# The a*b product of batch 1 rewritten as Strassen's seven block products

## Chip, cores and metric

One core of one Trainium2 chip runs the whole program. The metric is device time in microseconds (us), the median of several runs. TensorE (PE in the rows; its weight loads are PEld), VectorE (DVE), ScalarE (ACT) and GpSimd (POOL) each work through their own queue in order; SyncE (SP) issues the transfers.

## What is computed

An attention layer over 2 batches of 576 tokens, 8 heads of 64, gives x (1152 x 512). Then follow a bilinear layer and a mixture of four experts:

```python
a = x @ w1            # 512 -> 1024
b = x @ w2
h = a * b @ w3        # 1024 -> 1024
x = h @ w_out         # 1024 -> 512
for e in range(4):
    out += p[:, e:e+1] * (np.maximum(x @ e_w1[e], 0) @ e_w2[e])
```

Everything is float32. The kernel reaches that with products of float32r halves: a value is split into a high part (a copy to float32r) and a low part (the value less its high part), and each product is made of three passes, low by high, high by low and high by high (`PASSES`, line 54). The high part is a copy on ScalarE or GpSimd, the low part a subtraction by `lo_dve` (line 107, VectorE) or `lo_pool` (line 104, GpSimd).

## The kernel before

The work comes in four stretches. **Stretch 1** holds the attention of both batches (eight pairs of heads, p = 0 to 3 for batch 0, 4 to 7 for batch 1), the product of w3 and w_out (`wacc`, line 471) and a*b of batch 0 (`b0`, line 596). Its order is written out by hand in the list `FIRST` (lines 19 to 48), where each word is a part: `s`, `t`, `v`, `n`, `z` are TensorE's work for attention, `w` and `b` that for the weights' product and for a*b, the others are the conversions between on the other engines, `@` a load. `manual_schedule` (line 660) keeps every engine's queue in that order. The parts `z4` to `z7` transpose batch 1's attention output into PSUM; `zh4` to `zh7` copy it as the high part (line 398, ScalarE), `zl4` to `zl7` subtract for the low part (line 401, VectorE).

**Stretch 2**, the last words of `FIRST` (`k00_0` to `kc31`), is c of batch 0: hT (a*b split in two) times the product of w3 and w_out, 192 matmuls of line 615, with copies to `x2` (line 624).

**Stretch 3** is a*b of batch 1 (`b1`, lines 664 and 814 to 828): 16 units u, unit 2m for the m-th block of 128 columns of w1 and 2m+1 for that of w2, each times the two halves of 288 tokens over four blocks of 128 of the depth (line 541; 12 matmuls for a unit and half, 384 in all). The weights come back from DRAM, where batch 0 stored them as float32 (`wf`, lines 512 and 527), and are split by ScalarE and VectorE (line 532). An even unit's result is copied by ScalarE (`keep`, line 551); for an odd one VectorE multiplies (`times`, line 555), ScalarE copies the high part of hT (line 560), VectorE subtracts for the low part. The two banks are M0 and M1. c of batch 1 for the first 320 tokens (`c1`, lines 830 to 836) comes behind in the program, in banks o0 to o3, and was put by the scheduler between the units, 12 matmuls at a time.

**Stretch 4** is the four experts, whose first layer is already done by Strassen's seven products (`step`, lines 910 to 954, products of line 923). Its weights are prepared by `prep_1` (line 735): the high parts by ScalarE (line 751), the low parts and the four sums by GpSimd (lines 754 to 764).

The on-chip memory of attention (pools A1 and A2) is given up at line 666, and the pool `px` of stretch 4 takes its place.

## Time and profile before

| | |
|---|---|
| median of 3 runs | 694.44 us (694.14 to 694.61) |
| profiled execution, its own time | 694.88 us |
| its span, first to last instruction | 693.0 us |
| instructions | 12797 |
| busy in the span: PE, PEld | 98%, 88% |
| busy in the span: DVE, ACT, POOL | 60%, 54%, 51% |
| TensorE's granted clock | 1.000 of full speed throughout |

The profile is of one execution. Busy time is the time in which an engine had an instruction running; matmuls overlap, so a busy PE is not yet a PE at its full rate. In the rows further down, a line number is that of the code above, `x24` is a count of instructions, and the text in brackets behind an instruction is the idle time of its engine ahead of it and who ended it.

### The profile page before, as it was taken

The page shows a single profiled execution, that of the slowest core. Times are in us where ns is not written, and L with a number is a line of the kernel's source. Part 1 is how long each engine was busy: PE and PEld are TensorE (multiplying, and loading weights), DVE is VectorE, ACT ScalarE, POOL GpSimd, SP SyncE. Part 2 cuts the span into 40 slices and gives each one's busy share as a digit, 9 for nine tenths or more (in the row PEclk, how much of TensorE's full clock was granted, in tenths as well). Part 3 has the DMA queues.
Part 4 walks back from the last instruction along what each step waited for, and adds up shares of the span by engine and source line. Part 5 has one row for each costly group of instructions (what it writes and reads, how often), then busy time and mean ns, then how long its engine had stood idle before and what let it go on. Part 6 is the DMA issues. An engine that isn't in the chain of part 4 may idle for free.

```text
span 693.0 us, 12797 instructions
## 1 busy us (share of the span) xinstructions
PE 682.0 (98%) x4925; PEld 611.7 (88%) x4925; DVE 416.7 (60%) x784; ACT 370.8 (54%) x785; POOL 354.4 (51%) x350
## 2 busy tenths in 40 slices
PE   8999999999999999999999999999999999999997
PEld 5777798888999999999899998889999898999896
DVE  6788788998851144457766563456563465544563
ACT  6896787576741234355454544445544545544551
POOL 2034645565530001416777766668765668666660
PEclk9999999999999999999999999999999999999999
DMA  9556265534540014112222331231323132313401
GB/s 283 180 160 217 72 197 183 175 108 125 180 138 31 1 61 130 54 61 93 69 85 78 105 122 62 68 116 63 121 83 100 61 111 72 123 61 94 164 31 61
DMA packets 43404, 74.53 MB, mean 108 GB/s; under 512 B 14416, under 2 KB 14416, under 8 KB 43344
## 3 DMA queue, kind: packets, MB, share of 16 engines
q1 hardware_dynamic: 43344, 73.72, 32.9%
q8 instruction: 39, 0.64, 0.4%
q14 instruction: 21, 0.17, 0.1%
HBM read 67.15 MB, written 6.55 MB: 106 GB/s over the span
## 4 chain that ended last, share of the span: by engine, by line
PE 87%; DVE 6%; ACT 3%; DMA 2%; issue 1%; POOL 0%; SPq 0%; ACTq 0%; DVEq 0%; POOLq 0%
PE o L876 28%; PE Z L923 14%; PE ab L541 13%; PE c L615 7%; PE Q L923 7%; PE wacc L471 6%; PE R L923 3%; PE a L329 2%; PE pt L306 2%; PE sc L252 2%; ACT P L273 1%; DVE P L268 1%; DMA wr<-in_moe_w_tiles_dram 1%; DMA qd<-in_q_cols_dram 1%; PE b L363 1%
## 5 line engine op out<-in xcount | busy, mean ns | idle before, releaser
L104 POOL TENSOR_TENSOR w<-r,w 128x512 fp32r<-128x512 f32 x96 | 130.5, 1360 | 188.4 <-ACT w L751 183.2
L876 PE MATMUL o<-w,he 128*128 128x512 f32 x864 | 224.0, 392 | 0.0
L876 PEld LDWEIGHTS o<-w,he 128*128 128x128 f32 x864 | 153.6, 188 | 23.8
L541 PE MATMUL ab<-xT,ws 128*128 128x288 f32 x768 | 108.0, 297 | 2.1 <-POOL ws L104 1.7
L861 ACT ACTIVATE he<-t 128x320 fp32r<-128x320 f32 (+1 forms) x96 | 42.7, 445 | 121.0 <-DVE t L952 73.5
L541 PEld LDWEIGHTS ab<-xT,ws 128*128 128x128 f32 x768 | 103.1, 188 | 4.2 <-POOL ws L104 2.6
L862 DVE SCALAR_TENSOR_TENSOR he<-t,he 128x320 fp32r<-128x320 f32 (+1 forms) x96 | 57.2, 595 | 49.1 <-ACT he L861 49.1
L107 DVE TENSOR_TENSOR w<-r,w 128x512 fp32r<-128x512 f32 x64 | 66.5, 1040 | 0.0
L945 DVE TENSOR_TENSOR t<-u,Q 128x320 f32<-128x320 f32 (+1 forms) x32 | 14.6, 455 | 82.8 <-ACT u L943 82.7
L751 ACT CAST w<-r 128x512 fp32r<-128x512 f32 x96 | 58.9, 614 | 0.0
L615 PE MATMUL c<-hT,W 128*128 128x288 f32 (+2 forms) x384 | 52.9, 295 | 0.0
L615 PEld LDWEIGHTS c<-hT,W 128*128 128x128 f32 x384 | 51.6, 188 | 0.0
L923 PE MATMUL Z<-X0T,w 128*128 128x320 f32 x288 | 50.3, 310 | 0.3 <-ACT s L933 0.3
L923 PEld LDWEIGHTS Z<-X0T,w 128*128 128x128 f32 x288 | 46.2, 188 | 4.2 <-ACT s L933 0.7
L471 PE MATMUL wacc<-wo,w3s 128*128 128x512 f32 x192 | 48.2, 400 | 0.0
L923 PEld LDWEIGHTS Z<-X1T,w 128*128 128x128 f32 x288 | 41.0, 189 | 4.0
L471 PEld LDWEIGHTS wacc<-wo,w3s 128*128 128x128 f32 x192 | 35.0, 188 | 8.8 <-issue 1.0
L923 PE MATMUL Z<-X1T,w 128*128 128x256 f32 x288 | 42.1, 282 | 0.0
L268 DVE CUSTOM_DVE_ANT_0 P<-sc,mask 128x128 f32<-128x128 f32 (+4 forms) x72 | 33.7, 515 | 10.9 <-PE sc L252 6.4
L781 ACT CAST w<-r 128x512 fp32r<-128x512 f32 x64 | 39.5, 618 | 0.0
L273 ACT ACTIVATE P<-P,mn 128x128 f32<-128x128 f32 (+4 forms) x72 | 37.5, 579 | 1.2 <-DVE mn L268 1.1
L101 POOL TENSOR_SCALAR w3s<-tf_l 128x512 fp32r<-128x512 f32 x16 | 12.5, 780 | 45.3 <-DVE tf_l L137 34.3
(136 smaller groups left out, 1157.0 us busy)
## 6 DMA issues: line engine op xcount, KB each, us to landing
r<-in_moe_w_tiles_dram SPq DMA_DIRECT2D x64, 256.0 KB, 3.6
r<-in_moe_w_dram SPq DMA_DIRECT2D x64, 256.0 KB, 3.1
w3r<-in_moe_w_tiles_dram SPq DMA_DIRECT2D x16, 512.0 KB, 3.6
wr<-in_moe_w_tiles_dram SPq DMA_DIRECT2D x16, 512.0 KB, 4.0
wor<-in_moe_w_out_dram SPq DMA_DIRECT2D x8, 512.0 KB, 4.3
wf<-tf SPq DMA_DIRECT2D x16, 256.0 KB, 4.2
wr<-wf SPq DMA_DIRECT2D x16, 256.0 KB, 2.9
qd<-in_q_cols_dram SPq DMA_DIRECT2D x8, 352.0 KB, 4.1
```

Of the source, the lines that this page charges most:

```text
L104: nc.gpsimd.tensor_sub(dst, src, r32(hi))
L107: nc.vector.tensor_sub(dst, src, r32(hi))
L268: nc.vector.tensor_tensor_reduce(out=Pt[i, x], in0=src, in1=mask[:, 0:S] if i == NB else mask[:, S + P - w : S + P], scale=ISCALE, scalar= ...
L273: nc.scalar.activation(Pt[i, x], Pt[i, x], AF.Exp, bias=one, scale=-1.0)
L471: nc.tensor.matmul(wacc[u], lhsT=w3s[u][:, a, c, :], rhs=wo[4 * g + c][:, bb, :], start=(c == 0 and x == 0), stop=(c == 3 and x == 2),)
L541: nc.tensor.matmul(ps[:, 0:HS], lhsT=self.ws[u][:, wi, kk, :], rhs=xT[b, kk][:, xi, a * HS : (a + 1) * HS], start=(n == 0), stop=(n == 3 * ...
L615: nc.tensor.matmul(st["ps"], lhsT=Wt[kk][:, wi, d * P : (d + 1) * P], rhs=hT[kk][:, xi, t0 : t0 + tw], start=(kk == 0 and x == 0), stop=(k ...
L751: return lambda: nc.scalar.copy(st["w"][i][:, 0], src(i))
L861: nc.scalar.activation(h[:, 0], src, AF.Relu)
L862: nc.vector.scalar_tensor_tensor(out=h[:, 1], in0=src, scalar=0.0, in1=r32(h[:, 0]), op0=ALU.max, op1=ALU.subtract)
L876: nc.tensor.matmul(o_ps[i], lhsT=h_of[s][x][:, a, i * P : (i + 1) * P], rhs=w2s[s][x][:, b, :], start=first, stop=last,)
L923: nc.tensor.matmul(ps, lhsT=w1s[s][a][:, wi, kk, :], rhs=X[c, b][:, xi, kk, :], start=first and kk == 0 and x == 0, stop=(kk == 1 and x == ...
```

## The change

a*b of batch 1 is computed as Strassen's seven products of 2 x 2 blocks. For each m the left block matrix is made of the m-th columns of w1 and w2, each cut in two along the depth (A11, A12 from w1, A21, A22 from w2); the right one of x, cut in two along the depth and in two along the tokens. Each product is two blocks deep, three passes each, on 288 tokens: 6 matmuls; seven products make 42 for each m, 336 in all. Results are gathered in Z, Q and R (`b1_prods`): three copies by ScalarE (`keep`), three sums by VectorE (`add`), then two multiplications, one copy of the high part (576 wide) and one subtraction for the low part (`fin_h`). Even m use banks M0, M1 and o0, odd m o1, o2 and o3.

The weights are prepared by the `prep_1` of stretch 4 with other arguments: four high parts on ScalarE, four low parts and the two sums of `s24` on VectorE, the two sums of `s31` still on GpSimd. Three sets of tiles are used in turn; the sets for m = 0 to 2 and all of x's blocks (`x_b1`) are made beside c of batch 0 (stretch 2 behind the word `rl71`), two pieces of work behind each word of c; the sets for m = 3 to 7 within the loop, set m+2 beside the products of m from m = 1 on. Batch 1's attention output is now kept as float32 (`xf`), so `zl4` to `zl7` go.

`FIRST` is written anew: the same parts but for those four, in another order. In stretch 1 the loads of weights keep their order but for a few places, `w8` to `w10` come ahead of `s61`, and `z7` comes between `b15_0` and `b15_1`. Only the expert blocks X1B11 and X1B21 (256 tokens) are still split early; X0B11, X0B21 and the first expert's weights follow behind the last products, since their memory is lent to the products.

```diff
 
 
     raw_t, qk_t, phi_t, prob_t = {}, {}, {}, {}
+    xf = []
     halves = (slice(0, SB), slice(SB, P))
 
     mz = A1.tile([P, G, 2, D + 1], F32, name="mz")
@@ -380,8 +381,8 @@
             nc.gpsimd.tensor_add(st["q"], st["q"], st["m"])
 
         def fin():
-            if b:
-                xT[b, h // 2] = main.tile([P, 2, S], F32R, tag=f"g{p}", name=f"xT{b}_{h // 2}")
+            if b and h % 4 == 0:
+                xf.append(main.tile([P, 2, S], F32, tag=f"g{H // 2 + len(xf)}", name=f"xf{len(xf)}"))
 
             st["x"] = ps = psS.tile([P, 1024], F32, tag="S", name=f"x{p}")[:, 0:S]
             for i in range(NB):
@@ -395,10 +396,11 @@
                 nc.tensor.matmul(ps[o, NB * P :], lhsT=st["q"][:, NB], rhs=identF[:, o], start=True, stop=True)
 
         def fin_hi():
-            nc.scalar.copy(xT[b, h // 2][:, 0, :], st["x"])
+            nc.scalar.copy(xf[h // 4][:, h // 2 % 2, :] if b else xT[b, h // 2][:, 0, :], st["x"])
 
         def fin_lo():
-            lo_dve(xT[b, h // 2][:, 1, :], st["x"], xT[b, h // 2][:, 0, :])
+            if b == 0:
+                lo_dve(xT[b, h // 2][:, 1, :], st["x"], xT[b, h // 2][:, 0, :])
 
         parts.update({
             f"n{p}": mem, f"g{p}": mem_out, f"v{p}0": pv(0), f"v{p}1": pv(1), f"v{p}2": pv_last, f"j{p}": join,
@@ -505,12 +507,6 @@
-            if self.b:
...
-                nc.sync.dma_start(out=self.raw[u], in_=wf[u])
-                return
...
@@ -562,30 +558,6 @@
-        def mm(self, u, a):
...
-        def start(self):
...
-        def unit(self, u):
...
@@ -657,12 +629,11 @@
             fs = c_unit(0, d, a * HS, HS, ps_main(d, a))
             parts.update({f"k{d}{a}_{q}": f for q, f in enumerate(fs[:4])})
             parts[f"kc{d}{a}"] = fs[4]
+    cut_at = max(i for i, f in enumerate(FIRST) if f[0] != "k") + 1
     with tc.manual_schedule(engines=ENGINES | {ET.SP}):
-        for f in FIRST:
+        for f in FIRST[:cut_at]:
             parts[f]()
 
-    b1 = BUnits(1, nc.scalar.copy, lo_dve)
-    b1.start()
     attn.close()
 
     p3 = ctx.enter_context(ExitStack())
@@ -671,7 +642,13 @@
 
 
     BL = ("B11", "B21", "T1", "T2", "T3", "T4")
-    X = {(c, n): px.tile([P, 2, 2, w], F32R, name=f"X{c}{n}") for c, (_, w) in enumerate(COLS) for n in (*BL, "B22")}
+
+    def x_tiles(c, names):
+        for n in names:
+            X[c, n] = px.tile([P, 2, 2, COLS[c][1]], F32R, tag=f"X{c}{n}", name=f"X{c}{n}")
+
+    X = {}
+    x_tiles(1, BL[:2])
     t3 = px.tile([P, 2, COLS[0][1]], F32, name="t3")
     px.tile([P, SHIFT], F32, name="gapx")
 
@@ -732,15 +709,15 @@
             pools[i].tile([P, 2, n, P], F32R, tag=f"v{i}", name=f"w1{i}_{s}") for i, n in enumerate(SIZES)
         ]
 
-    def prep_1(s):
+    def prep_1(s, raw=raw1, out=w1s, tiles=None, nm="t1", low=lo_pool, eng=nc.gpsimd):
 
         st = {}
 
         def begin():
-            st["r"] = raw1.pop(s)
-            st["t"] = px.tile([P, 2, P], F32, tag="t1", name=f"t1_{s}", bufs=2)
-            st["w"] = set_of(s)
-            w1s[s] = dict(zip(("A11", "A12", "S2", "S4", "S1", "A22", "S3"), (
+            st["r"] = raw.pop(s)
+            st["t"] = px.tile([P, 2, P], F32, tag="t1", name=f"{nm}_{s}", bufs=2)
+            st["w"] = (tiles or set_of)(s)
+            out[s] = dict(zip(("A11", "A12", "S2", "S4", "S1", "A22", "S3"), (
                 st["w"][i][:, :, k : k + 2] for i in range(4) for k in ((0, 2) if i < 3 else (0,))
             )))
 
@@ -751,7 +728,7 @@
             return lambda: nc.scalar.copy(st["w"][i][:, 0], src(i))
 
         def lo(i):
-            return lambda: lo_pool(st["w"][i][:, 1], src(i), st["w"][i][:, 0])
+            return lambda: low(st["w"][i][:, 1], src(i), st["w"][i][:, 0])
 
         def s31():
             a11, a21, a22 = st["r"][:, 0, 0:2], st["r"][:, 1, 0:2], st["r"][:, 1, 2:4]
@@ -760,8 +737,8 @@
 
         def s24():
             a11, a12, s1 = st["r"][:, 0, 0:2], st["r"][:, 0, 2:4], st["r"][:, 1, 0:2]
-            nc.gpsimd.tensor_sub(a11, s1, a11)
-            nc.gpsimd.tensor_sub(a12, a12, a11)
+            eng.tensor_sub(a11, s1, a11)
+            eng.tensor_sub(a12, a12, a11)
 
         return {
             "s31": s31, "s24": s24, "begin": begin,
@@ -805,25 +782,154 @@
         nc.vector.reciprocal(prs, prs)
         nc.vector.tensor_mul(pr, pr, prs.unsqueeze(2).to_broadcast([P, NTT, E]))
 
-    hT.clear()
-    early = [f for k, n in enumerate(("B11", "B21")) for c in range(2) for f in split_x(n, c, block(0, k, c))]
-    p0 = prep_1(0)
-    early += [
-        lambda: (p0["begin"](), p0["hi0"]()), *(p0[n] for n in ("lo0", "s31", "hi2", "hi3", "s24", "lo2", "hi1", "lo3", "lo1")),
-    ]
+    BX = {}
+    b1_raw, b1_set = {}, {}
+
+    def load_b1(m):
+        if m < KF:
+            b1_raw[m] = r = px.tile([P, 2, KD, P], F32, tag=f"X{m % 2}B22", name=f"wr1_{m}")
+            for x in range(2):
+                nc.sync.dma_start(out=r[:, x], in_=wf[2 * m + x])
+
+    def b1_tiles(m):
+        if m % 3 == 0:
+            return [px.tile([P, 2, n, P], F32R, tag=f"v{i}", name=f"b1w{i}_{m}") for i, n in enumerate(SIZES)]
+        c = m % 3 - 1
+        return [px.tile([P, 2, n, P], F32R, tag=f"X{c}{BL[2 + i]}", name=f"b1w{i}_{m}") for i, n in enumerate(SIZES)]
+
+    def prep_b1(m):
+
+        p = prep_1(m, b1_raw, b1_set, b1_tiles, "tb", lo_dve, nc.vector)
+        return [
+            [p["begin"], p["hi0"], p["s31"]], [p["lo0"]], [p["s24"], p["hi3"]], [p["hi2"], p["lo3"]], [p["lo2"], p["hi1"]],
+            [p["lo1"], lambda: load_b1(m + 2)], [],
+        ]
+
+    def x_b1():
+
+        x0, x1 = xf
+        t = pf.tile([P, 2, HS], F32, tag="asb", name="xt", bufs=1)
+        lft, rgt = slice(0, HS), slice(HS, S)
+        b11, b12, b21, b22 = x0[:, :, lft], x0[:, :, rgt], x1[:, :, lft], x1[:, :, rgt]
+        where = {
+            "B11": (main, "g6"), "T1": (main, "g7"), "B21": (main, "g2"), "B22": (main, "g3"), "T2": (px, "X0B11"),
+            "T3": (px, "X0B21"), "T4": (main, "g4"),
+        }
+
+        def hi(n, src):
+            def f():
+                pool, tag = where[n]
+                BX[n] = pool.tile([P, 2, 2, HS], F32R, tag=tag, name=f"BX{n}")
+                nc.scalar.copy(BX[n][:, 0], src)
+            return f
+
+        def lo(n, src):
+            return lambda: lo_dve(BX[n][:, 1], src, BX[n][:, 0])
+
+        sub = nc.vector.tensor_sub
+        return [
+            hi("B11", b11), lambda: sub(t, b12, b11), lo("B11", b11), hi("T1", t), lambda: sub(b12, b22, b12), lo("T1", t),
+            hi("B21", b21), hi("B22", b22), lambda: sub(t, b22, t), lo("B21", b21), hi("T2", t), lo("B22", b22),
+            hi("T3", b12), lo("T2", t), lambda: sub(b21, b21, t), lo("T3", b12), hi("T4", b21), lo("T4", b21),
+        ]
+
+    st_m = {}
+
+    def b1_prods(m):
+
+        st_m[m] = st = {}
+        banks = ((psM, "M0"), (psM, "M1"), (ps3, "o0")) if m % 2 == 0 else ((ps3, "o1"), (ps3, "o2"), (ps3, "o3"))
+
+        def new(i):
+            pool, tag = banks[i]
+            return pool.tile([P, 512], F32, tag=tag, name=f"{'ZQR'[i]}b{m}", bufs=1)[:, 0:HS]
+
+        def prod(d, a, b, first):
+            def f():
+                if first:
+                    st[d] = new("ZQR".index(d))
+                for kk in range(2):
+                    for x, (wi, xi) in enumerate(PASSES):
+                        nc.tensor.matmul(
+                            st[d], lhsT=b1_set[m][a][:, wi, kk, :], rhs=BX[b][:, xi, kk, :],
+                            start=first and kk == 0 and x == 0, stop=(kk == 1 and x == 2), skip_group_check=True,
+                        )
+            return f
+
+        def keep(i):
+            def f():
+                if i == 0:
+                    st["u"] = pf.tile([P, 3, HS], F32, tag="ws", name=f"u{m}")
+                nc.scalar.copy(st["u"][:, i], st["Z"])
+            return f
+
+        def add(i, k, d):
+            def f():
+                if i == 0:
+                    st["t"] = pf.tile([P, 3, HS], F32, tag="raw", name=f"t{m}")
+                nc.vector.tensor_add(st["t"][:, i], st["u"][:, k], st[d])
+            return f
+
+        def fin_h(a):
+            def f():
+                t = st["t"]
+                nc.vector.tensor_mul(t[:, a], t[:, a], st["Z"] if a == 0 else t[:, 2])
+                if a:
+                    hT[m] = po.tile([P, 2, S], F32R, tag=f"o{m}", name=f"hT1_{m}")
+                    both = t[:, 0:2].rearrange("p a s -> p (a s)")
+                    nc.scalar.copy(hT[m][:, 0, :], both)
+                    lo_dve(hT[m][:, 1, :], both, hT[m][:, 0, :])
+            return f
+
+        return {
+            "P1": [prod("Z", "A11", "B11", True), keep(0)], "P2": [prod("R", "A12", "B21", True), add(0, 0, "R")],
+            "P6": [prod("Z", "S2", "T2", False), keep(1)], "P5": [prod("Q", "S1", "T1", True)],
+            "P7": [prod("Z", "S3", "T3", False), keep(2), add(2, 2, "Q")], "P4": [prod("Z", "A22", "T4", False), fin_h(0)],
+            "P3": [prod("Q", "S4", "B22", False), add(1, 1, "Q"), fin_h(1)],
+        }
+
+    tail = FIRST[cut_at:]
+    work, ahead = [], [fs for m in range(3) for fs in prep_b1(m)]
+    for f in x_b1():
+        work += [f, *(ahead.pop(0) if ahead else [])]
+    work += [f for fs in ahead for f in fs]
     with tc.manual_schedule(engines=ENGINES | {ET.SP}):
-        for u in range(NU):
-            pre, m0, m1, post = b1.unit(u)
-            pre()
-            if u == 6:
+        load_b1(0), load_b1(1)
+        per = -(-len(work) // max(1, sum(f[1] != "c" for f in tail)))
+        for f in tail:
+            parts[f]()
+            if f[1] != "c":
+                for g in work[:per]:
+                    g()
+                work = work[per:]
+        for g in work:
+            g()
+        hT.clear()
+        early = [f for k, n in enumerate(("B11", "B21")) for f in split_x(n, 1, block(0, k, 1))]
+        p0 = prep_1(0)
+        early += [
+            lambda: (p0["begin"](), p0["hi0"]()), *(p0[n] for n in ("lo0", "s31", "hi2", "hi3", "s24", "lo2", "hi1", "lo3", "lo1")),
+        ]
+        order = [b1_prods(m) for m in range(KF)]
+        for n in ("P1", "P5", "P2"):
+            for f in order[0][n]:
+                f()
+        for m in range(KF):
+            todo = prep_b1(m + 2) if m and m + 2 < KF else []
+            if m == 4:
                 load_1(0), load_1(1)
-            m0()
-            if u >= 3 and early:
-                early.pop(0)()
-            m1()
-            post()
-            if u >= 8 and early:
-                early.pop(0)()
+            nxt = order[m + 1] if m + 1 < KF else {}
+            seq = [order[m].get("P6"), *([order[m]["P5"]] if m else []), order[m]["P7"], nxt.get("P1"), order[m]["P4"], nxt.get("P2"), order[m]["P3"]]
+            for fs in seq:
+                for f in fs or []:
+                    f()
+                for f in todo.pop(0) if todo else []:
+                    f()
+                if early and (m == KF - 1 or m == KF - 2 and len(early) > 10):
+                    early.pop(0)()
+        x_tiles(0, BL[:2])
+        for k, n in enumerate(("B11", "B21")):
+            early += split_x(n, 0, block(0, k, 0))
         for f in early:
             f()
 
@@ -835,6 +941,8 @@
         for f in c1(d, 0, d):
             f()
     px.tile([P, SHIFT], F32, name="gapy")
+    for c in range(2):
+        x_tiles(c, (*BL[2:], "B22"))
     c1_rest = [f for d in range(KD) for f in c1(d, 1, (KD + d) % 5)]
     p2.close()
 ```

## Rows read from the trace of the kernel before

**Rows 1.** The page, part 1: busy time, share of the span, instructions.
```profile
PE 682.0 (98%) x4925; PEld 611.7 (88%) x4925; DVE 416.7 (60%) x784; ACT 370.8 (54%) x785; POOL 354.4 (51%) x350
```

**Rows 2.** Busy by stretch: PE, PEld, DVE, ACT, POOL (counts), clock, DMA share, GB/s.
```profile
0.00:208.50 208.50, 201.57 (x1949) 168.72 (x1950) 169.76 (x385) 149.86 (x291) 93.39 (x94) 1.00 0.54 168
208.50:234.10 25.60, 25.60 (x195) 25.60 (x194) 1.59 (x4) 3.75 (x9) 0.00 (x0) 1.00 0.07 22
234.10:297.20 63.10, 63.10 (x470) 63.10 (x468) 27.06 (x48) 24.65 (x54) 9.38 (x10) 1.00 0.21 68
```

**Rows 3.** The chain that ended last, 208 to 262 us: start, length, what.
```profile
208.72 25.44 PE c L615 x192
234.16 9.54 PE ab L541 x72
...
253.57 6.37 PE ab L541 x48
```

**Rows 4.** The chain that ended last, one stretch of the attention's time.
```profile
168.87 0.05 DVE P L268
...
172.65 1.87 PE ab L541 x12
```

**Rows 5.** VectorE on batch 1's attention output, 100 to 209 us (min/median/max ns; first and last start).
```profile
L107 DVE TENSOR_TENSOR xT<-x,xT x4: 749/754/758, 151.2 to 203.0; 128x576 fp32r<-128x576 f32 x4
```

**Rows 6.** Busy by stretch, columns as in rows 2.
```profile
140.00:160.00 20.00, 20.00 (x151) 16.90 (x150) 19.17 (x35) 15.82 (x29) 13.11 (x12) 1.00 0.37 119
```

**Rows 7.** Groups by shape, 210 to 297 us: busy us, mean ns of one | idle before.
```profile
L555 DVE TENSOR_TENSOR asb<-ab,asb 128x288 f32<-128x288 f32 x15 | 6.9, 457 | 15.6 <-PE ab L541 15.6
L551 ACT COPY asb<-ab 128x288 f32<-128x288 f32 x16 | 6.4, 399 | 10.7 <-PE ab L541 9.8 <-DVE hT L107 0.3
L759 POOL TENSOR_TENSOR r<-r 128x256 f32<-128x256 f32 x2 | 1.4, 727 | 0.0
```

**Rows 8.** Instructions in order of time in stretch 3: start, length, engine, line.
```profile
249.17 0.43 ACT L560 CAST hT<-asb 128x288 fp32r<-128x288 f32 x1 [0.54 <-DVE asb L555]
249.51 0.62 ACT L532 CAST ws<-wr 128x512 fp32r<-128x512 f32 x1
249.63 0.46 DVE L107 TENSOR_TENSOR hT<-asb,hT 128x288 fp32r<-128x288 f32 x1 [0.50 <-ACT hT L560]
250.16 0.69 DVE L107 TENSOR_TENSOR ws<-wr,ws 128x512 fp32r<-128x512 f32 x1
...
250.77 0.82 DVE L107 TENSOR_TENSOR X0B<-x,X0B 128x640 fp32r<-128x640 f32 x1
```

**Rows 9.** Instructions in order of time, 319 to 334 us.
```profile
319.74 0.22 DVE L805 RECIPROCAL prs<-prs 128x9 f32<-128x9 f32 x1
319.99 0.44 DVE L806 TENSOR_TENSOR pr<-pr,prs 128x36 f32<-128x36 f32 x1
...
332.75 0.42 ACT L933 COPY s<-Z 128x320 f32<-128x320 f32 x1
...
333.22 0.88 PEld L923 LDWEIGHTS Z<-X0T,w 128*128 128x128 f32 x6 [0.69 <-ACT s L933]
```

**Rows 10.** Groups by shape, VectorE, 340 to 693 us.
```profile
L107 DVE TENSOR_TENSOR w<-r,w 128x512 fp32r<-128x512 f32 x60 | 62.7, 1046 | 0.0
...
L945 DVE TENSOR_TENSOR t<-u,Q 128x256 f32<-128x256 f32 x16 | 6.8, 422 | 36.2 <-ACT u L943 36.2
```

**Rows 11.** Instructions in order of time, GpSimd and VectorE, 146 to 148 us.
```profile
146.24 1.28 POOL L104 TENSOR_TENSOR w3s<-tf_l,w3s 128x512 fp32r<-128x512 f32 x1
146.32 1.75 DVE L136 SCALAR_TENSOR_TENSOR tf_l<-tf_l,tu_l 128x512 uint32<-128x512 uint32 x1
```

**Rows 12.** Batch 1's weights coming back from DRAM, 195 to 300 us: time to landing.
```profile
DMA to landing us min/median/max: 2.5/2.9/4.7
```

More of the change, by code (lines that the diff above doesn't have):

```diff
@@ L45 @@
[L45 to L48 removed]
+@q0 @k0 @k1 @q1 e0 @V0 f0 s00 s01 @w0 m00 e1 m01 s02 x00 @o0 f1 s03 @V1 x01 m02 wa0 t00 @k2 t02 m03 @q2 s10 x02 wd0
@@ new lines @@
+@w1 s11 c00 wp0 c02 t01 m10 @o1 x03 t04 c01 s12 @o2 c04 m11 x10 t03 m12 v00 @mz c03 x11 t05 @bt v01 c05 x12 t06 t10
+s13 c06 c10 e2 v02 m13 @q3 oa0 t14 gates j0 @k3 t13 c14 n0 @V2 x13 od0 t11 s20 g0 c11 @o3 wa1 t12 m20 v10 ja0 c12 c13
+x20 t16 v11 f2 oh0 wd1 t15 e3 s21 c15 ol0 @w2 c16 oa1 v12 m21 wp1 w0_0 j1 @V3 x21 s22 od1 s23 m22 t20 oa2 @w3 t22 m23
+c20 n1 @k4 x22 od2 @q4 z0 c22 g1 @w4 t24 x23 t21 c24 s30 f3 c21 zh0 t23 oa3 ja1 m30 t25 c23 zl0 v20 c25 od3 x30 v21
+@w5 oh1 t26 oh3 n2 ol1 c26 oh2 ol3 wa2 v22 ol2 g2 w0_1 hq4 @V4 w0_2 hk4 lq4 j2 s31 e4 w0_3 m31 lk4 s32 y0 x31 wd2 z1
@@ L49 @@
+rm70 rh70 b15_1 zh7 rl70 k00_0 rm71 rh71 k00_1 rl71 k00_2 k00_3 k01_0 kc00 k01_1 k01_2 k01_3 k10_0 kc01 k10_1 k10_2
+k10_3 k11_0 kc10 k11_1 k11_2 k11_3 k20_0 kc11 k20_1 k20_2 k20_3 k21_0 kc20 k21_1 k21_2 k21_3 k30_0 kc21 k30_1 k30_2
+k30_3 k31_0 kc30 k31_1 k31_2 k31_3 kc31
 """.split()
@@ L564, in h_lo @@
             lo_dve(hT[m][:, 1, sl], self.asb[m][:, a, :], hT[m][:, 0, sl])
-        def mm(self, u, a):
-            self.product(u, a)
-            if u % 2:
-                for f in (self.times, self.h_hi, self.h_lo):
-                    f(u // 2, a)
-            else:
-                self.keep(u, a)
-        def start(self):
-            for u in range(self.ahead):
-                self.load(u)
-            self.conv(0), self.conv(1)
-        def unit(self, u):
-            def pre():
-                if u + self.ahead < NU:
-                    self.load(u + self.ahead)
-            def post():
-                if u + 2 < NU:
-                    self.conv(u + 2)
-            return [pre, lambda: self.mm(u, 0), lambda: self.mm(u, 1), post]
     def gates():
```

52 lines of the change are left out of this document (20 added, 32 removed).

## The prediction

> **What bounds the kernel now.** I read the busy time first, then the stretches, then the chain of waits, and last the instructions in order of time. TensorE is busy for 98% of the span, the other three for 51 to 60% [rows 1]. That is an average of unlike stretches. In the first 208.5 us VectorE runs for 169.8 us and TensorE's rate is uneven; then come 25.6 us for c of batch 0, in which TensorE has no gap, VectorE has 1.6 us of work and GpSimd none; then 63.1 us for a*b of batch 1 with most of c's first half for batch 1 between, again without a gap on TensorE, while VectorE has 27.1 us of work, ScalarE 24.7 and GpSimd 9.4 [rows 2]. The chain says the same: through both of these stretches it is TensorE's matmuls end to end [rows 3]. So a matmul saved there is worth its time, as long as the other engines keep up, and the question of this change is whether they do.
>
> The rate: 48 matmuls of a*b take 6.37 us in the chain [rows 3], 0.1327 us each. The 384 of batch 1 take 50.96 us.
>
> **What is removed.** 336 matmuls of the same width stand in for 384; 48 times 0.1327 is 6.37 us. That is all that can be won in the loop, and only if no product waits.
>
> **What is added beside c of batch 0.** VectorE gets seven low parts and four differences of x, 576 wide, 0.754 us each [rows 5]; back to back an independent instruction starts 0.08 us before the one ahead ends (0.69 us long, the next 0.61 us later) [rows 8], so 11 x 0.67 = 7.4 us. Each of three weight sets adds three low parts of 512 (0.61 each), one of 256 and two sums of 256 (0.42 long [rows 10]; the second sum reads the first, and a dependent instruction starts 0.03 us after the end of the one before [rows 9]): 1.83 + 0.34 + 0.34 + 0.45 = 2.96, for three 8.9 us. With the 1.6 us that are there it makes 17.9 us in 25.6. If GpSimd's six sums of 0.73 us [rows 7] stopped VectorE for their whole length, 4.4 us more, 22.3. ScalarE: seven copies of 576 (about 0.67, between the 0.43 for 288 and 0.62 for 512 [rows 8] carried on), and per set three of 0.62 and one of about 0.40, each less 0.09 back to back: 4.1 + 5.7 us, beside its 3.75. All of it fits; the first weights land some 2.9 us after their issue [rows 12], which the 25.6 us also hold, and the last block, T4, is first read by the seventh product, 4.8 us into the loop. I cost it at nothing; TensorE's c hides it, and every microsecond by which a set or block came later than that would be one of the path. The transfers on SyncE's queue keep their number and size (two of 256 KB for each m); the first two now wait for attention's memory, and nothing urgent stands behind them.
>
> **The loop, one turn.** For m = 1 to 5 a turn holds seven products of 6 matmuls, 7 x 0.796 = 5.57 us, and VectorE's and ScalarE's queues in the order of the diff: `keep`, `hi0`, `lo0`, `keep`, `add`, `s24` (two), `hi3`, `hi2`, `lo3`, `mul`, `lo2`, `hi1`, `add`, `lo1`, `add`, `mul`, copy, low part. I count from the end of the second `mul` of turn m-1, called 0.
> - ScalarE copies 576 from 0.03 to 0.70 (hop of 0.03 us [rows 8]), and only behind that `keep` of product P6: 0.61 to 1.01 (0.40 each [rows 7]). P7 adds to the same bank, so it starts 0.05 us after that copy's end (the hop [rows 9]), at 1.05, though P6 and P5 had long ended.
> - TensorE then runs P7, P1 of the next m, P4, P2, P3 to 5.03. `add` and `mul` (0.46 each [rows 7]) follow: 5.08 to 6.03. If VectorE were free, a turn would take 6.03 us.
> - VectorE stands idle until ScalarE's copy is there, as it does now for 0.50 us behind every copy [rows 8]; low part at 0.73, `lo0` at 1.57 (`hi0` ends at 1.54), `add` at 2.33 (behind `keep` of P7), the sums at 2.71 and 3.16, `lo3` 3.50, `mul` 3.84, `lo2` 4.22, `add` 4.83, `lo1` 5.21, `add` 5.82, `mul` 6.31 to 6.77.
>
> So VectorE, not TensorE, sets the turn: 6.77 us against 5.57.
>
> **The loop's sum.** Start: three products, 2.39; P6 0.80; P7 waits 0.5 for the copy of P6 just ahead of it; five products, 3.98: P3 of m = 0 ends at 7.66 and its `mul` 1.00 later. Five turns of 6.77 bring 42.51, turn 6 without a set 6.03 more, 48.54; the last: 1.05 and three products, 2.39: 51.98. Against 50.96 this is **+1.0 us**: the saved matmuls are eaten whole.
>
> **GpSimd in the loop.** The sums of `s31` for sets 5 to 7 run when their weights land, within turns 2 to 4; those of sets 3 and 4 near the end of c. Beside GpSimd, VectorE's subtraction of 512 takes 1.05 us on average where it takes 0.69 alone [rows 8, 10]; one instruction that began just after a GpSimd instruction of 1.28 us took 1.75 [rows 11], 0.55 us beyond the other's end, so it did not share but stood still. The Trainium skill, page "SBUF — State Buffer", section "Who interferes with whom", says that a VectorE instruction with two SBUF inputs and a GpSimd one that reads SBUF exclude each other for the whole instruction. The trace agrees [rows 11], and by that rule the six sums here could cost their full length. Lower bound: nothing, where they fall beside an addition with a PSUM input or in VectorE's idle 0.7 us; upper bound: 6 x 0.73 = 4.4 us. VectorE works on two SBUF inputs for some 4 us of the 6.77; about a third of the upper bound, **+1.5 us**, seems nearest.
>
> **Behind the loop.** c's first half for batch 1, 96 matmuls, was put between the units and now follows in one piece, since its banks are lent to the products; its time stays. It hides the last hT (1.0 + 0.70 + 0.79 us after P3, needed only after 21 matmuls of 0.14 us), X0B11, X0B21 and the first expert's set (GpSimd, eight instructions, some 8 us, begun in the last turn). Without this cover they would cost their length. Bank o0 comes free a turn early, so up to 18 of the 96 can fill the waits of the last turn: between 0 and -1.5 us, I take **-0.5**.
>
> **The first 208 us.** Four VectorE instructions of 0.754 us go [rows 5]. VectorE is busy for 19.17 of 20 us where the first lies [rows 6], and the chain later leaves TensorE for VectorE from 168.87 to 172.65 [rows 4]; what is taken off that queue before then shortens the path by up to 1.4 us, what is taken off after 172.65 by nothing. The rest of the new order is the same work in other places, and I see no reason for a sum of one sign; its bound is one such stretch of 3.8 us more or less. I take **-1.0**.
>
> **Sum.** +1.0 + 1.5 - 0.5 - 1.0 = +1.0 us. The profiled execution took 694.88 us, 1.88 around its span of 693.0; the median of the runs is 694.44, so 0.44 lower. On the median: 695.4 us, no change that a measurement here can tell (0.2%, 1.4 us).
>
> **The rivals.**
> 1. VectorE keeps up, and only ScalarE's copy delays P7. For it: the waits I put in VectorE's row add up to 1.0 us a turn, and could lie elsewhere. Against: its instructions alone fill 5.7 us. Then the turn is 6.03: 5 x 0.74 less, and GpSimd costs nothing: 695.4 - 3.7 - 1.5 = 690.2 us. With no wait at all it would be some 687.
> 2. Slower: GpSimd's six sums each stop VectorE for their length, in the turns where it sets the pace. It decides as soon as the weights of sets 5 to 7 land while VectorE is between two SBUF subtractions; `s31` starts by itself then. 4.4 in place of 1.5: 698.3 us. The stop seen beside GpSimd [rows 11] speaks for it, the additions from PSUM against.
> 3. The order of the first 208 us wins or loses a stretch like that of [rows 4]: 691.6 or 699.2 us.
>
> That the products are not fewer can be left out: the counts are fixed by the code.
>
> **How the numbers follow.** The forecast's own case (turns of 6.5 to 7.3 us, range 693.3 to 697.6) gets 0.50: same 0.30, slower 0.17, faster 0.03. Rival 1 gets 0.22, all faster; rival 2 0.15, all slower; rival 3 0.13: faster 0.05, same 0.02, slower 0.06. Faster 0.30, same 0.32, slower 0.38. The range, 690.0 to 698.5, takes in rivals 1 and 2 and leaves out the far ends of rival 3 and a loop without waits.
>
> **What would show it.** Right: 336 matmuls for a*b of batch 1 in place of 384, the loop at about 52 us with TensorE idle before P7 once a turn, VectorE's busy share there near 85%, c of batch 0 still 25.4 us and unbroken. The chain would change between VectorE, ScalarE and TensorE in every turn. Wrong: a loop near 45 us (products without waits), a gap between c and the first products (preparation late), VectorE's 512 subtractions at over 1 us in the loop (rival 2), or a start of c that moved by over 2 us (rival 3).

## The result, and the profile after

The changed kernel takes 699.00 us, the median of four runs (698.25 to 700.15), against 694.53 us (694.14 to 694.77) for the kernel before beside it: a ratio of 1.0066 [1.0048, 1.0084], slower by 4.5 us. That lies just above the range of the forecast, 690.0 to 698.5. The profiled execution took 699.71 us with a span of 697.9, where the one before took 694.88 with 693.0: 4.9 us more in the span, and the pages and stretches below account for it.

In the rows of the kernel after, L853 is a product, L863 `keep`, L870 `add`, L876 `mul`, L880 ScalarE's copy of hT, L728 the high part of a weight block, L740 and L741 the two sums of `s24` on VectorE, L735 and L736 the two of `s31` on GpSimd, L107 a low part on VectorE, and L587 a matmul of c.

The page of the kernel after, busy time and share of the chain by engine:

```profile
PE 677.8 (97%) x4877; PEld 606.0 (87%) x4877; DVE 448.1 (64%) x839; ACT 383.5 (55%) x808; POOL 369.2 (53%) x366
...
PE 83%; DVE 9%; ACT 4%; issue 1%; DMA 1%; POOL 0%; DVEq 0%; ACTq 0%; POOLq 0%
```

Against [rows 1] there are 48 matmuls fewer and 55 VectorE instructions more, and TensorE is busy for 4 us less in a span 5 us longer. So the products are fewer, as the code says, and TensorE now waits. Busy time by stretch says where (kernel after; columns as in [rows 2]):

```profile
0.00:208.97 208.97, 200.25 (x1950) 167.88 (x1951) 164.77 (x380) 149.97 (x291) 94.00 (x94) 1.00 0.52 162
208.97:234.40 25.43, 25.43 (x194) 25.43 (x193) 21.38 (x31) 12.65 (x26) 7.46 (x8) 1.00 0.34 110
234.40:303.60 69.20, 61.81 (x434) 60.42 (x433) 44.66 (x82) 30.16 (x65) 18.59 (x20) 0.98 0.17 57
260.00:280.00 20.00, 16.40 (x110) 15.94 (x110) 16.13 (x33) 9.62 (x21) 3.08 (x4) 0.91 0.24 80
```

Row by row against [rows 2]: c of batch 0 starts 0.4 us later (208.97 where it was 208.56 in the trace); c itself is as long as before and has no gap, though VectorE now works for 21.4 us of it where it did for 1.6; and the third stretch, up to the first product of the experts, has 7.4 us in which TensorE stands. The kernel before reached that product with 12 of c's matmuls (1.75 us) still to come; counted with them, the way from c's start to the experts grew from 90.39 us to 94.64, by 4.25 us. Between 260 and 280 us, in the middle of the loop, VectorE is busy for 81% of the time and TensorE's granted clock is 0.91 (last row), where [rows 2] have 1.00 in all three stretches.

The chain that ended last is what the loop looks like from the end. One whole turn of the kernel after, from one copy of hT to the next (start, length, what):

```profile
249.97 0.47 DVE t L876
...
250.46 0.67 ACT hT L880
251.13 0.31 ACT u L863
...
251.48 1.08 PE Zb L853 x6
...
253.39 0.62 DVE wr L740
...
254.03 0.85 DVE wr L741
...
257.55 0.47 DVE t L876
...
258.04 0.67 ACT hT L880
258.71 0.31 ACT u L863
...
259.06 1.07 PE Zb L853 x6
```

Where [rows 3] showed matmuls end to end, here only one product in seven is on the chain (the one that waits); the rest is the last `mul`, ScalarE's 576-wide copy, the `keep` queued behind it (L863), and then VectorE's own row of instructions up to the next `mul`. From copy to copy it is 7.58 us for 5.57 us of matmuls. The copies start at 243.50, 250.46, 258.04, 265.60, 273.34 and 281.48, so turns 1 to 5 last 6.96, 7.58, 7.56, 7.74 and 8.14 us, where the forecast had 6.77 and a share of GpSimd's time.

The same turn in order of time shows why it is 7.58 and not 6.96 (kernel after; start, length, engine, line). The first two rows are the same two subtractions one turn earlier:

```profile
246.42 0.42 DVE L740 TENSOR_TENSOR wr<-wr 128x256 f32<-128x256 f32 x1
246.88 0.42 DVE L741 TENSOR_TENSOR wr<-wr 128x256 f32<-128x256 f32 x1
...
251.48 1.06 PE L853 MATMUL Zb<-BXT,b1w 128*128 128x288 f32 x6 [1.11 <-ACT u L863]
...
252.58 0.40 ACT L863 COPY u<-Zb 128x288 f32<-128x288 f32 x1 [0.63 <-PE Zb L853]
...
252.98 0.74 POOL L735 TENSOR_TENSOR tb<-wr 128x256 f32<-128x256 f32 x1 [15.39 <-DMA wr<-wf]
253.02 0.46 DVE L870 TENSOR_TENSOR t<-u,Qb 128x288 f32<-128x288 f32 x1 [0.34 <-ACT u L863]
...
253.39 0.61 DVE L740 TENSOR_TENSOR wr<-wr 128x256 f32<-128x256 f32 x1
...
253.80 0.80 POOL L736 TENSOR_TENSOR wr<-wr 128x256 f32<-128x256 f32 x1
...
254.03 0.85 DVE L741 TENSOR_TENSOR wr<-wr 128x256 f32<-128x256 f32 x1
...
266.62 1.07 PE L853 MATMUL Zb<-BXT,b1w 128*128 128x288 f32 x6 [1.72 <-ACT u L863]
...
274.36 1.32 PE L853 MATMUL Zb<-BXT,b1w 128*128 128x288 f32 x6 [1.88 <-ACT u L863]
275.48 1.64 PE L853 MATMUL Zb<-BXB,b1w 128*128 128x288 f32 x6
276.92 1.61 PE L853 MATMUL Zb<-BXT,b1w 128*128 128x288 f32 x6
278.36 0.97 PE L853 MATMUL Rb<-BXB,b1w 128*128 128x288 f32 x6
```

Beside GpSimd's two sums the subtractions take 0.61 and 0.85 us in place of 0.42, 0.62 us together. VectorE's ends each come 0.28 us after GpSimd's (254.00 after 253.72, 254.88 after 254.60), though the first pair overlaps for 0.33 us and the second for 0.57. Had VectorE gone on at a lower rate, the longer overlap would have left less to do behind it; so I read it as standing until the other is done. The weights of sets 5, 6 and 7 land in turns 2, 3 and 4, and these are the turns that are 0.60 to 0.78 longer.

One more row is worth a look: P7 (251.48) lasts 1.06 us from its start to the end of its last matmul, as the profile models that end. The `keep` that reads it starts at 252.58, 1.10 us behind P7's start, and the `add` behind that at 253.02, 2.59 us behind the end of the last `mul`.

The last four rows show something that no step of the prediction had asked about. Turns 2, 3 and 4 each end in a wait of TensorE's before the next P7, of 1.73, 1.72 and 1.88 us; in turn 5, which has no sums of GpSimd, the products behind that wait take 1.6 us where they take 0.96 elsewhere. The granted clock there (kernel after, columns as in [rows 2]):

```profile
274.30:276.00 1.70, 1.64 (x9) 1.64 (x10) 1.19 (x2) 0.81 (x3) 0.00 (x0) 0.69 0.00 0
276.00:278.00 2.00, 2.00 (x10) 2.00 (x10) 1.55 (x4) 1.21 (x4) 0.00 (x0) 0.50 0.01 4
278.00:280.00 2.00, 2.00 (x16) 2.00 (x15) 1.43 (x4) 0.65 (x2) 0.00 (x0) 0.91 0.02 4
```

At 276 to 278 us it is 0.50, the 1.2 GHz level, and it is back at the 2.4 GHz level before 280. Turn 5 is 8.14 us long, 1.2 more than turn 1, which like it has no sums beside it.

### The profile page after: what moved, and what is told of

The parts are those of the page before. It is cut to its first block, busy times and chain, and to the rows that moved or that the text cites. A ratio compares the mean times of both kernels' runs of the same rounds, so it can differ in the third digit from the quotient of the medians.

```text
span 697.9 us, 12801 instructions
## 1 busy us (share of the span) xinstructions
PE 677.8 (97%) x4877; PEld 606.0 (87%) x4877; DVE 448.1 (64%) x839; ACT 383.5 (55%) x808; POOL 369.2 (53%) x366
## 4 chain that ended last, share of the span: by engine, by line
PE 83%; DVE 9%; ACT 4%; issue 1%; DMA 1%; POOL 0%; DVEq 0%; ACTq 0%; POOLq 0%
PE o L984 27%; PE Z L1031 14%; PE c L587 7%; PE Q L1031 7%; PE wacc L473 6%; PE ab L537 6%; PE R L1031 3%; PE Zb L853 3%; PE a L330 2%; PE pt L307 2%; PE sc L253 1%; DVE P L269 1%; ACT P L274 1%; DVE b1w L107 1%; DMA wr<-in_moe_w_tiles_dram 1%
## 5 line engine op out<-in xcount | busy, mean ns | idle before, releaser
L104 POOL TENSOR_TENSOR w<-r,w 128x512 fp32r<-128x512 f32 x96 | 131.7, 1372 | 126.4 <-ACT w L728 126.4
L107 DVE TENSOR_TENSOR w<-r,w 128x512 fp32r<-128x512 f32 x64 | 66.3, 1036 | 0.0
L537 PE MATMUL ab<-xT,ws 128*128 128x288 f32 x384 | 55.7, 299 | 2.1 <-POOL ws L104 1.4
L537 PEld LDWEIGHTS ab<-xT,ws 128*128 128x128 f32 x384 | 51.6, 188 | 3.9 <-POOL ws L104 2.9
L587 PE MATMUL c<-hT,W 128*128 128x288 f32 (+2 forms) x384 | 52.6, 295 | 0.0
L587 PEld LDWEIGHTS c<-hT,W 128*128 128x128 f32 x384 | 51.5, 188 | 0.0
```

Source lines behind the costliest of these rows:

```text
L104: nc.gpsimd.tensor_sub(dst, src, r32(hi))
L107: nc.vector.tensor_sub(dst, src, r32(hi))
L537: nc.tensor.matmul(ps[:, 0:HS], lhsT=self.ws[u][:, wi, kk, :], rhs=xT[b, kk][:, xi, a * HS : (a + 1) * HS], start=(n == 0), stop=(n == 3 * ...
L587: nc.tensor.matmul(st["ps"], lhsT=Wt[kk][:, wi, d * P : (d + 1) * P], rhs=hT[kk][:, xi, t0 : t0 + tw], start=(kk == 0 and x == 0), stop=(k ...
```

## The experiments

My theory, Theory A in the expectations, was the forecast's with three prices corrected: VectorE's row of instructions, with ScalarE's copy of hT ahead of `keep` in the queue, sets the turn; GpSimd's sums stop VectorE for part of their length in turns 2 to 4; the clock falls as a result of the waits; and the new order of the first 208 us costs time by itself. The rivals are told in each expectation. The kernel before took 694.49 us beside e1 to e4 and 694.43 beside e5 to e8.

**e1: without GpSimd's sums for sets 5 to 7.**

```diff
-    def prep_1(s, ..., low=lo_pool, eng=nc.gpsimd):
+    def prep_1(s, ..., low=lo_pool, eng=nc.gpsimd, sums=True):
...
         def s31():
+            if not sums:
+                return
...
-        p = prep_1(m, b1_raw, b1_set, b1_tiles, "tb", lo_dve, nc.vector)
+        p = prep_1(m, b1_raw, b1_set, b1_tiles, "tb", lo_dve, nc.vector, m < 5)
```

> Left out: the two sums of s31 for the weight sets 5, 6 and 7 (the products S1 and S3 of those m take unsummed weights). Theory A (VectorE sets the turn, and GpSimd's two sums stop it for part of their length in three turns): the turns, P7 to P7, go from 6.95, 7.58, 7.56, 7.74 us to 6.95 in each; the run gets 2.0 us shorter, near 697.0, and with shorter waits TensorE's clock may keep its full level, 1 us more. Rival (the longer turns come from the transfers that land there, or from TensorE's waits alone): turns stay at 7.6 us, time unchanged.

Measured: 696.22 us (695.87 to 696.9), ratio 1.0026 [1.0016, 1.0035], 2.8 less than the kernel after. In order of time, kernel e1:

```profile
258.37 1.07 PE L855 MATMUL Zb<-BXT,b1w 128*128 128x288 f32 x6 [1.11 <-ACT u L865]
...
260.27 0.42 DVE L742 TENSOR_TENSOR wr<-wr 128x256 f32<-128x256 f32 x1
260.73 0.42 DVE L743 TENSOR_TENSOR wr<-wr 128x256 f32<-128x256 f32 x1
```

The subtractions are 0.42 again, and turns 1 to 5 are 6.96, 6.96, 6.97, 6.97 and 6.96 us. The wait before P7 is 1.11 us in turns 2 to 5, and the clock does not fall. The transfers of these sets still run in turns 2 to 4, so they are not the cause. So six instructions on an engine that is idle for most of this stretch cost 2.0 us by holding VectorE (0.62 + 0.60 + 0.78), and the clock's 1.2 us in turn 5 go with them; the profiled executions differ by 3.4 us, the medians by 2.8. What is left, 6.96, is the turn without GpSimd: 0.19 more than I had put together.

**e5: without VectorE's low parts of sets 3 to 7.**

```diff
         p = prep_1(m, b1_raw, b1_set, b1_tiles, "tb", lo_dve, nc.vector)
+        if m >= 3:
+            p.update({f"lo{i}": lambda: None for i in range(4)})
...
-                            st[d], lhsT=b1_set[m][a][:, wi, kk, :], rhs=BX[b][:, xi, kk, :],
+                            st[d], lhsT=b1_set[m][a][:, wi if m < 3 else 0, kk, :], rhs=BX[b][:, xi, kk, :],
```

> Left out: VectorE's four low parts of the weight sets 3 to 7 (the products of those m use the high part in their place). The order is that of the changed kernel. Theory A (VectorE's queue sets the turn; ScalarE's copy of hT ahead of P7's copy is the next limit): turns of 6.2 us, between the 5.57 of the matmuls and the 6.95 measured, with a wait of some 0.4 to 0.5 us before P7 left in each; 692 us. Rival (the place of ScalarE's copy alone sets the turn): turns stay near 7, 698 to 699. Rival (TensorE's matmuls are the next limit): turns of 5.6, 689.

Measured: 693.52 us (693.12 to 694.27), ratio 0.999 [0.9981, 0.9999]. TensorE in order of time, kernel e5:

```profile
251.50 1.06 PE L855 MATMUL Zb<-BXT,b1w 128*128 128x288 f32 x6 [0.45 <-ACT u L865]
...
257.80 1.06 PE L855 MATMUL Zb<-BXT,b1w 128*128 128x288 f32 x6 [0.45 <-ACT u L865]
```

All five turns are 6.30 us, as expected to 0.1, the ones beside GpSimd's sums too. The sums hold VectorE here for less, as only the first subtraction is lengthened, from 0.42 to 0.48, 0.62 and 0.81 us; and with the slack that VectorE has, even the 0.39 us of the longest hold cost the turn nothing. The time lies 1.5 us above the 692 of the sum: in this profile c starts 0.7 us later than in the kernel after, and turn 6 is 0.3 longer (8.22 for 7.89). The other 0.7 us over the matmuls is the wait (P7 starts 1.41 us behind the start of the product ahead, not 0.80, and the next one 0.90 behind P7), and what it waits for is the `keep` behind the copy of hT (e2 and e6 move that copy). So the turn of the kernel after is made of three layers: matmuls 5.6, the copy in the queue 0.7, VectorE's row 0.66, and on top of them GpSimd's 0.6 to 0.8 in three turns.

**e2: the copy of hT one place later.** ScalarE's copy is queued behind the next turn's first `keep` and `hi0`, VectorE's low part of it behind `s24` and `hi3`.

```diff
-                if a:
-                    hT[m] = po.tile([P, 2, S], F32R, tag=f"o{m}", name=f"hT1_{m}")
-                    ...
+            "H": h_copy, "L": h_low,
...
-            for fs in seq:
+            for i, fs in enumerate(seq):
...
+                if m and i == 0:
+                    order[m - 1]["H"]()
+                if m and i == 2:
+                    order[m - 1]["L"]()
```

> Same work; hT's copy on ScalarE is queued behind the next turn's first copy of Z, and its low part on VectorE behind the next turn's two sums. Theory A: P7 no longer waits for VectorE's last multiplication through ScalarE, and VectorE no longer stands 0.74 us for that copy; a turn falls to VectorE's own work, about 5.9 us (6.5 with GpSimd's sums beside it) in place of 6.95 to 7.7. Over five turns 5 us less, and 1.2 more if the clock holds: 693 to 694.5 us. Rival (VectorE's amount of work alone sets the turn, waits are filled anyway): turns of 6.7 to 7.4, at most 1.5 us less, 697.5.

Measured: 694.41 us (693.66 to 694.78), ratio 0.9997 [0.9988, 1.0007], 4.6 less than the kernel after. The time is at the upper end of what was expected, 693 to 694.5; the turns are not where they were expected, at 5.9 and 6.5, but at 6.29, 6.80, 6.80, 6.81 and 6.08 us. Three of the five are those of the rival (6.7 to 7.4). The five are 5.2 us shorter than in the kernel after, 1.2 of it the clock, where 6.2 had been counted. In order of time, kernel e2:

```profile
257.69 0.67 ACT L884 CAST hT<-t 128x576 fp32r<-128x576 f32 x1 [1.38 <-DVE t L876]
258.27 0.39 ACT L863 COPY u<-Zb 128x288 f32<-128x288 f32 x1
...
258.71 1.08 PE L853 MATMUL Zb<-BXT,b1w 128*128 128x288 f32 x6 [0.96 <-ACT u L863]
...
259.86 0.75 DVE L107 TENSOR_TENSOR hT<-t,hT 128x576 fp32r<-128x576 f32 x1
...
260.30 0.91 POOL L735 TENSOR_TENSOR tb<-wr 128x256 f32<-128x256 f32 x1 [5.02 <-DMA wr<-wf]
...
260.53 0.96 DVE L107 TENSOR_TENSOR b1w<-tb,b1w 128x256 fp32r<-128x256 f32 x1
```

P7 no longer waits, but the copy now stands ahead of the second `keep`, and P4, which adds to the bank that this one clears, waits 0.96 us in P7's place. The wait moved by one product. The last two rows are GpSimd's hold again, on another instruction: 0.96 us in place of 0.42, ended 0.28 us after GpSimd's end.

**e3: idle matmuls in the wait.** Six matmuls into a free bank, whose result nothing reads, are queued behind P5.

```diff
+        def idle():
+            ps = ps3.tile([P, 512], F32, tag="o4", name=f"idle{m}")[:, 0:HS]
+            ...
-            "P6": ..., "P5": [prod("Q", "S1", "T1", True)],
+            "P6": ..., "P5": [prod("Q", "S1", "T1", True), *([idle] if m else [])],
```

> Added: six matmuls into an unused bank ahead of P7 in the turns 1 to 7, 0.8 us each turn, within a wait of 1.1 to 1.9 us in turns 2 to 5 (0.45 in turn 1). Theory A with a clock that falls because TensorE waited: the granted clock stays at 1.00 through the loop, turn 5 loses its extra 1.2 us, and the run is 0 to 1.0 us shorter (turns 6 and 7, which had little wait, give some back). Rival (the clock falls for another reason, or its fall costs nothing as VectorE sets the turn): clock falls again or the time is 0.5 to 1.6 us longer.

Measured: 699.90 us (699.79 to 700.26), ratio 1.0078 [1.0063, 1.0093]: a miss in the sum, 0.9 longer than the kernel after, as the rival had it (0.5 to 1.6 longer). The clock did what the theory says (kernel e3, columns as in [rows 2]):

```profile
274.00:282.00 8.00, 7.46 (x55) 7.47 (x56) 6.51 (x13) 4.68 (x11) 0.00 (x0) 1.00 0.01 2
```

It stays at the 2.4 GHz level, and turn 5 is 6.97 us in place of 8.14, with the same instructions on VectorE. The mean granted clock of its four runs is 0.999 to 1.000, where the kernel after has 0.995 to 0.998. The waits that are left before P7 in turns 2 to 5 are 0.31 to 1.10 us. So 1.2 us of the kernel after's profiled execution are the clock, and with the waits shortened, by e1 or by e3, the fall is gone: it came of TensorE's waits. The price was on the other side: in turns 6 and 7, where c's own matmuls fill the wait, the idle ones came on top (8.35 and 8.76 us for 7.89 and 7.51).

**e4 and e8: the order of the first 208 us.** e4 is the kernel after with the order of before (without the four low parts of X1 that the change removes); e8 is the kernel before with the new order (and these four put back, each behind its high part). Both edit only the string of the order, of which the first line that differs is shown; e8's diff is the same the other way round.

```diff
-@q0 @k0 @k1 @q1 e0 @V0 f0 s00 s01 @w0 m00 e1 m01 s02 x00 @o0 f1 s03 @V1 x01 m02 wa0 t00 @k2 t02 m03 @q2 s10 x02 wd0
+@q0 @k0 @k1 @q1 e0 @V0 f0 s00 s01 @w0 m00 e1 m01 s02 x00 @V1 f1 s03 @o0 x01 m02 wa0 t00 @k2 t02 m03 @q2 s10 x02 wd0
...
```

> The changed kernel with the order of the first 208 us as it was before, less the four low parts that are gone. The new order's c of batch 0 started at 209.13 us, that of before at 208.72. Theory A (the new order costs a little, and taking four VectorE instructions off the old one gains up to 1.4 us): c starts at 207.3 to 208.7, the run is 0.4 to 1.8 us shorter, 697.2 to 698.6. Rival (the order is worth nothing, the loss is all in the loop): c starts at 209.1 and the time stays at 699.0.

> The kernel before with the new order of the first 208 us, the four low parts put back right behind their high parts. If the new order costs 1.1 us by itself (the changed kernel started c at 209.13, with the old order at 207.98): c starts at 209.5 to 210, 695.2 to 696.0 us. Rival (the order costs only together with the missing low parts, or with the new work behind it): c starts at 208.7 and the time is that of before, 694.5.

Measured: e4 697.31 us (697.21 to 697.88), ratio 1.0041 [1.0026, 1.0056], 1.7 less than the kernel after; e8 696.16 us (695.58 to 696.5), ratio 1.0024 [1.0013, 1.0034], 1.7 more than the kernel before. Where c of batch 0 starts, first in e4:

```profile
207.98 4.25 PE L587 MATMUL c<-hT,W 128*128 128x288 f32 x31
```

and in e8:

```profile
209.74 2.53 PE L615 MATMUL c<-hT,W 128*128 128x288 f32 x18
```

With the kernel before at 208.56 and the kernel after at 208.97 these are the four corners of a square: the new order costs 1.2 us with the low parts (209.74 to 208.56) and 1.0 without (208.97 to 207.98), and taking the low parts away gains 0.6 to 0.8. Each corner is one profile, though. Over all runs, five profiles with the new order and no low parts start c at 209.2 on average (208.88 to 209.65), three with the old order at 207.9 (207.47 to 208.34). Profiles that share order and low parts spread by 0.8 to 0.9 us, so the cost of the order is clear of it, and so are the 1.7 us of e8's median; the gain from the low parts is not (e5, which lacks them, starts c at 209.65, 0.09 before e8). Of e4's 1.7 us the start of c gives 1.0 and the loop's turns 1 to 5 another 0.6 (37.41 us for 37.98). Which wait of the new order costs it was not traced to one place.

e4 also tells something of the clock. TensorE in order of time, kernel e4:

```profile
250.52 1.07 PE L853 MATMUL Zb<-BXT,b1w 128*128 128x288 f32 x6 [1.11 <-ACT u L863]
...
258.25 1.11 PE L853 MATMUL Zb<-BXT,b1w 128*128 128x288 f32 x6 [1.88 <-ACT u L863]
259.16 1.64 PE L853 MATMUL Zb<-BXB,b1w 128*128 128x288 f32 x6
260.60 1.64 PE L853 MATMUL Zb<-BXT,b1w 128*128 128x288 f32 x6
...
274.00 1.06 PE L853 MATMUL Zb<-BXT,b1w 128*128 128x288 f32 x6 [1.90 <-ACT u L863]
274.90 0.96 PE L853 MATMUL Zb<-BXB,b1w 128*128 128x288 f32 x6
```

Here it fell one wait into the slow turns, behind 1.88 us at 258, and not behind 1.90 us at 274; in the kernel after it held through 1.73 and 1.72 us and fell behind 1.88. So a wait of this length can cost the clock and need not (one run of e4 has a mean of 1.000, three 0.998), and there it cost less, since VectorE set that turn anyway (7.98 us).

**e6: another order in the loop.** The old order of the first 208 us; the weights' conversions stand ahead of the products they share a place with; ScalarE's copy of hT stands behind both `keep`s and VectorE's low part behind the `add`.

```diff
-            [p["begin"], p["hi0"], p["s31"]], [p["lo0"]], [p["s24"], p["hi3"]], [p["hi2"], p["lo3"]], [p["lo2"], p["hi1"]],
-            [p["lo1"], lambda: load_b1(m + 2)], [],
+        ] if m < 3 else [
+            [p["begin"], p["hi0"], p["s31"]], [p["lo0"], p["s24"]], [p["hi3"], p["hi2"], p["lo3"], p["lo2"]], [], [p["hi1"]],
+            [p["lo1"], lambda: load_b1(m + 2)], [],
...
-            "P7": [prod("Z", "S3", "T3", False), keep(2), add(2, 2, "Q")], "P4": [prod("Z", "A22", "T4", False), fin_h(0)],
+            "P7": [prod("Z", "S3", "T3", False), keep(2), later("H"), add(2, 2, "Q"), later("L")], "P4": [prod("Z", "A22", "T4", False), fin_h(0)],
```

> The whole work, correct: the order of the first 208 us as before less the four low parts; in the loop hT's copy is queued behind both copies of Z that the products wait for, the weights' conversions ahead of them, hT's low part behind the addition. Theory A: the turn is VectorE's amount of work, about 5.8 us, and 6.4 with GpSimd's sums beside it; c starts at 208.0. With the 694.4 of the run with the later copy less 1.1 (order) and 1.0 (three turns of 6.8 to 6.4): 692.3 us, faster than the kernel before. Rival (VectorE's amount is smaller than thought and the matmuls set the turn): 690. Rival (ScalarE's queue now delays the high parts and VectorE with them): 694.

Measured: 690.90 us (690.39 to 691.39), ratio 0.9952 [0.9936, 0.9969], 3.5 us faster than the kernel before and 8.1 faster than the kernel after, with the same instructions as the latter. In order of time, kernel e6:

```profile
249.32 0.68 ACT L887 CAST hT<-t 128x576 fp32r<-128x576 f32 x1
...
254.91 0.68 ACT L887 CAST hT<-t 128x576 fp32r<-128x576 f32 x1
...
256.68 0.73 POOL L735 TENSOR_TENSOR tb<-wr 128x256 f32<-128x256 f32 x1 [4.27 <-DMA wr<-wf]
256.79 1.23 DVE L107 TENSOR_TENSOR hT<-t,hT 128x576 fp32r<-128x576 f32 x1
...
263.15 1.08 PE L856 MATMUL Qb<-BXB,b1w 128*128 128x288 f32 x6 [0.38 <-DVE t L873]
```

Copy to copy is 5.59 us here and in the turn before: the matmuls set the turn, with no wait. I had expected 5.8 and 692.3 us; the rival in which the matmuls set the turn had 690. VectorE does the same work as in the kernel after, so there it was the order of the queues, and not VectorE's amount of work, that made a turn 6.96. The next two copies come 5.80 and 6.24 us apart, and the hold is again GpSimd's (1.23 us for a low part that takes 0.76 alone), now with less behind it.

**e7: e6 without GpSimd's sums for sets 5 to 7.** The edit is e1's, on e6.

```diff
-        p = prep_1(m, b1_raw, b1_set, b1_tiles, "tb", lo_dve, nc.vector)
+        p = prep_1(m, b1_raw, b1_set, b1_tiles, "tb", lo_dve, nc.vector, m < 5)
```

> The reordered kernel, with GpSimd's two sums for the weight sets 5 to 7 left out. Theory A (the lock costs some 0.65 us a turn while VectorE has no idle time): 1.5 to 2.0 us shorter than the reordered kernel, turns of 5.7 to 5.8. Rival (the order has left room for the sums): within 0.5 us of it.

Measured: 689.72 us (689.39 to 690.14), ratio 0.9933 [0.9919, 0.9948]. The first five copies of hT come 5.58 or 5.59 us apart, where e6 has 5.59, 5.59, 5.80 and 6.24. The sixth comes 7.78 us later (8.31 in e6), with 15 of c's matmuls between. So GpSimd's sums lengthen e6's loop by 1.4 us. The median is 1.2 us shorter than e6's, a little less than expected; its c started 0.9 us later than e6's (208.34 and 207.47), for no reason that the edit gives. What GpSimd's sums still cost in e6 is thus 1 to 2 us; moving them to a place where VectorE has no second SBUF input to wait for was not tried.

## Why the prediction was wrong

The mechanism was right in the loop: VectorE's row, with ScalarE's copy ahead of `keep`, sets the turn and eats the saved matmuls. The sum was wrong in five of its terms, four of them to the same side. Two were put at nothing without a reason that held: the clock, and the new order of the first 208 us. Three were mis-sized: the turn, by one link, GpSimd's hold, and c's matmuls in the waits. All are of the profiled execution, in us against the kernel before; the loop is counted from the first product (234.56) to the end of the last (295.85), less the 42 matmuls of c within it at 0.146: 55.2 us.

| term | forecast | measured | shown by |
|---|---|---|---|
| the loop without GpSimd (51.98 against 50.96) | +1.0 | +2.2 | e1: turns of 6.96 |
| GpSimd's sums | +1.5 | +2.0 | e1, and e5 for the slack |
| the clock | none | +1.2 | e3: turn 5 at 6.97 |
| c's matmuls in the waits | -0.5 | -1.2 | turns 6 and 7 |
| the first 208 us | -1.0 | +0.4 | start of c; e4 and e8 |
| what is left (mostly the time after the loop) | 0 | +0.3 | |
| sum | +1.0 | +4.9 | |

- **Beside c of batch 0**: right. I put VectorE at 17.9 to 22.3 us of work in it; it had 21.4, and c stayed unbroken at 25.43.
- **The loop, one turn**: the row was right, link by link, up to one: `add` behind `keep` of P7, which I had at 2.33 and which starts at 2.59. I had counted P7 at the 0.80 us by which products follow each other; its last matmul ends 1.06 us after its start, and what waits for it waits that long. Everything behind it is late by as much, less 0.07. The same link makes rival 1's 6.03 the 6.30 of e5. Five turns of 0.19 make 0.95 us, the start 0.25 more (the first copy 8.94 us after the first product, where I had 8.69). "VectorE, not TensorE, sets the turn" holds for this order of the queues alone: e6 does the same work in 5.59 us, so that the 5.7 us at which rival 1 put VectorE's instructions was a little too high.
- **GpSimd in the loop**: the failed step is "about a third of the upper bound". Which sets' sums lie in the loop I had said, three in turns 2 to 4; each two hold the turn for 0.6 to 0.8 us of their 1.5, nearly half. It goes the way [rows 11] had it: the later one stands still. The Trainium skill, page "SBUF — State Buffer", section "Who interferes with whom", says that the loser of this lock blocks fully and does not share; the trace agrees, with ends 0.28 us after GpSimd's in all three cases shown. Its full price, 4.4 us, was not paid, since VectorE had idle time or a PSUM input beside part of each.
- **Behind the loop**: c's matmuls gave more than twice what I took, and the limit of -1.5 holds. Turns 6 and 7 last 15.40 us with 42 of them (6.13); without them, by the forecast's rows, they would have been 6.03 and 4.47, so 1.2 us lay in the waits.
- **The first 208 us**: the -1.0 for the removed low parts was too much, as the corners of the square give 0.6 to 0.8 and that is not clear of the spread between profiles. "I see no reason for a sum of one sign", counted as nothing, was the larger error: the new order costs 1.0 to 1.2 us by itself. In place of -1.0 c starts 0.4 us later.
- **The clock**: no step of the prediction has it. The granted clock was 1.00 in every stretch of before that I read, and I forecast waits of 0.5 to 1 us in each turn without asking what they do to TensorE's clock. It fell once, behind the 1.88 us before turn 5, and cost 1.2 us; with waits of 1.11 us it did not fall (e1).

Of the rivals, the first (VectorE keeps up, 6.03 a turn) is refuted by e1 and e5. The other two came near in their numbers by luck. The second (GpSimd's full lock, 698.3) had 4.4 us for a hold that cost 2.0. The third (the new order loses a stretch of 3.8 us, 699.2) came nearest, and had the sign right, but the order costs 1.0 to 1.2 us. The rest is the clock and the longer turn.

What stays open: the cost of the clock in each run (the four runs of the kernel after spread over 1.9 us, their mean clocks of 0.995 to 0.998 do not rank them, since a run of 0.996 is the fastest, and e4's fall lay in another turn), and the place at which the new order loses its 1.2 us.
